# Splitting one kv product of a fused attention and MLP kernel by pair member, with casts and norms spread anew

## The chip, the cores and the metric

The kernel runs on one core of one Trainium2 chip. The metric is the device time of one execution in microseconds (us). Each kernel is run several times beside the kernel before on the same chip. Engines: PE is TensorE's matmul side and PEld its weight loads, ACT is ScalarE, DVE is VectorE, POOL is GpSimd, SP is the engine that issues the loads. Names in the profile lines: Eq and Ek are the exponentials of q and k, va is v after its cast, kvn is kv after its norm (the division by the sums), tp are the transposed queries and qT their copy, xT is the copy of x. A bank is one of PE's accumulator banks.

## The reference, cut to what matters

```python
def _attn_ref(q, k, v):                 # (8 batches, 8 heads, 576 rows, 64)
    q_s = softmax(q, axis=-1)           # per row
    k_s = softmax(k, axis=2)            # per column, over the 576 rows
    kv  = einsum('bhsd,bhse->bhde', k_s, v)
    return einsum('bhsd,bhde->bhse', q_s, kv)

def _moe_ref(x, w_in, w_out, beta):     # x: (4608, 512), w_in: 512 x 2048
    h = x @ w_in
    g = h * (1.0 / (1.0 + np.exp(-beta * h)))
    return g @ w_out
```

The softmax calls stand for the five lines each that the reference spells out. Inputs and output are float32.

## The kernel before

The kernel works through nine chunks of 512 rows. For each it forms kv of the heads, x (queries times kv), h (x times the first weight), tanh and g, and acc (g times the second weight). Batches 0 and 1 have a path of their own, since their data and both weights must first be loaded. Heads are handled in two halves `g`. Within a half, pair member `a` selects the PE row tile, and member `c` selects which 64 of 128 output rows are used.

The parts that the change and the argument touch:

```python
def ekv_mm(b, g, o0=0, c0=0, c1=VW - 2):        # VH = 66, VW = 132
    for t in range(KT9):                        # 9 row blocks
        for a in range(2):
            r = slice(a * KR, (a + 1) * KR)
            nc.tensor.matmul(ekv[b, 2 * g + a][:, o0 : o0 + c1 - c0],
                             Ek[b][r, t, g]..., ve(b)[r, t, g, c0:c1], ...)
def eks_mm(b, g):                               # the sums alone, two columns
    ekv_mm(b, g, VW, D, VH)
...
# the head: batch 0, second half of heads
ekv_open(0, 1, ("X1", "K"))
eks_mm(0, 1)
x_group(0, (0,), ["X0", "A0"])
ev_cast(0, 1, 0, nc.gpsimd)
ev_cast(0, 1, 1, nc.vector, 0, 5)
ev_cast(0, 1, 1, nc.gpsimd, 5, KT9)
ekv_rk(0, 1)
ekv_mm(0, 1)
x_out(0, 0, nc.scalar)
eq_out(0, 1, nc.vector)
...
ekv_norm(0, 1, nc.vector, nc.scalar)
x_out(0, 1, nc.vector)
for i in range(2):
    unit_mm(0, i, 0, 1)                         # two h matmuls as filler
x_group(0, (1,), ["X0", "H0"])
for i in range(2, 4):
    unit_mm(0, i, 0, 1)
...
def batch_1():                                  # the program order on ACT matters below
    b_mm(32)                                    # 32 of batch 0's 64 acc matmuls
    eq_exp(1, 0); eq_exp(1, 1)                  # exponentials of q
    eq_sum(1, 0); eq_div(1, 0, nc.vector)
    for c in range(2): ek_exp(1, 0, c)          # exponentials of k, first heads
    b_mm(20)                                    # emits output copies of tiles 0 and 1 on ACT
    eq_sum(1, 1)
    eq_t(1, 0, "X0", None)
    ...
    ev_cast(1, 0, 1, nc.scalar, 0, 4)
    eq_div(1, 1, nc.vector)
    for c in range(2): ek_exp(1, 1, c)          # exponentials of k, second heads
    b_mm(3)
    ekv_mm(1, 0)                                # the first kv product of batch 1
    b_mm(1)                                     # emits the output copy of tile 2 on ACT
    eq_t(1, 1, "H2", None)
    ekv_rk(1, 0, D)
    ekv_norm(1, 0, nc.vector, nc.scalar)
    eq_out(1, 0, nc.vector)                     # copy of qT
    ...
    b_mm(4)
    x_group(1, (0,), ["X0", "H0"])
    ekv_mm(1, 1)                                # the second kv product of batch 1
```

The softmax here doesn't subtract the row's maximum and nothing guards it: scores larger than these inputs give would overflow.

## Time and profile before

| | kernel before |
|---|---|
| median of the first three runs | 283.3 us (283.15 to 283.39) |
| span of the profiled run | 281.6 us |
| PE, ACT, DVE, POOL busy | 97%, 60%, 56%, 25% |
| DMA, mean over the span | 184 GB/s; 374 to 407 in the slices from 7 to 42 us |
| largest PE gap after the head | 0.32 us, ahead of batch 1's first kv product |

PE is busy throughout, so there is little to gain except in the first 16 us (the head, up to the dense stream of h) and where batch 1 joins. The lines that show this stand in the prediction.

### The profile page before, as it was taken

The page shows a single profiled execution, that of the slowest core. Times are in us where ns is not written, and L with a number is a line of the kernel's source. Part 1 is how long each engine was busy: PE and PEld are TensorE (multiplying, and loading weights), DVE is VectorE, ACT ScalarE, POOL GpSimd, SP SyncE. Part 2 cuts the span into 40 slices and gives each one's busy share as a digit, 9 for nine tenths or more (in the row PEclk, how much of TensorE's full clock was granted, in tenths as well). Part 3 has the DMA queues.
Part 4 walks back from the last instruction along what each step waited for, and adds up shares of the span by engine and source line. Part 5 has one row for each costly group of instructions (what it writes and reads, how often), then busy time and mean ns, then how long its engine had stood idle before and what let it go on. Part 6 is the DMA issues. An engine that isn't in the chain of part 4 may idle for free.

```text
span 281.6 us, 4611 instructions
## 1 busy us (share of the span) xinstructions
PE 273.1 (97%) x1664; PEld 136.1 (48%) x1692; DVE 156.8 (56%) x283; ACT 167.6 (60%) x279; POOL 70.3 (25%) x120
## 2 busy tenths in 40 slices
PE   7899999999999999999999999999999999999995
PEld 3555444545444445444544444444444444444444
DVE  2967369977865475549564766466453334444401
ACT  4757368867965587557855785478454544444411
POOL 3368721540721063104510361027000000000000
PEclk9999999999999999999999999999999999999999
DMA  7999999889699908991699069905100201031112
GB/s 233 374 391 407 389 384 358 303 161 359 158 217 350 199 37 182 331 240 52 154 331 279 26 135 300 284 29 120 70 37 2 76 37 40 0 76 37 40 75 75
DMA packets 51559, 51.69 MB, mean 184 GB/s; under 512 B 21068, under 2 KB 41932, under 8 KB 51536
## 3 DMA queue, kind: packets, MB, share of 16 engines
q1 hardware_dynamic: 51360, 51.33, 61.4%
q8 instruction: 13, 0.21, 0.3%
q14 instruction: 10, 0.08, 0.1%
q10 hardware_dynamic: 144, 0.07, 0.1%
q0 software_dynamic: 32, 0.01, 0.0%
HBM read 38.28 MB, written 9.44 MB: 169 GB/s over the span
## 4 chain that ended last, share of the span: by engine, by line
PE 83%; DMA 13%; ACT 1%; issue 1%; SPq 1%; ACTq 0%
PE acc L511 40%; PE h L459 39%; DMA k<-in_k_dram 7%; DMA wo<-in_moe_w_out_dram 4%; DMA wi<-in_moe_w_in_dram 2%; PE kv L386 2%; PE x L410 2%; PE kv L258 0%; ACT Ek L230 0%; SPq L105 0%; ACT o L540 0%; SPq L117 0%; PE xt L424 0%; PE tp L217 0%; ACT va L152 0%
## 5 line engine op out<-in xcount | busy, mean ns | idle before, releaser
L473 DVE SCALAR_TENSOR_TENSOR g<-th,h 128x512 bf16<-128x512 bf16 x144 | 97.3, 685 | 97.2 <-ACT th L471 97.0
L471 ACT ACTIVATE th<-h,beta_h 128x512 bf16<-128x512 f32 x144 | 97.1, 689 | 84.6 <-PE h L459 81.6
L511 PE MATMUL acc<-w_out_b,g 128*128 128x512 bf16 (+2 forms) x590 | 142.8, 368 | 1.7 <-issue 1.1
L459 PE MATMUL h<-xT,w_in_b 128*128 128x512 bf16 x503 | 127.4, 379 | 0.7 <-DVE xT L166 0.3
L459 PEld LDWEIGHTS <-w_in_b 128*128 128x128 bf16 x576 | 64.9, 113 | 61.1 <-issue 0.5
L511 PEld LDWEIGHTS <-g 128*128 128x128 bf16 x608 | 56.9, 98 | 63.9 <-issue 2.5
L317 POOL TENSOR_TENSOR Eq<-Eq,qz 128x512 bf16<-128x512 bf16 x24 | 25.1, 1048 | 84.4 <-issue 41.0
L540 ACT ACTIVATE o<-acc 128x512 f32<-128x512 f32 x34 | 20.0, 591 | 8.9 <-PE acc L511 7.4
L161 POOL TENSOR_SCALAR_AFFINE_SELECT va<-v 128x256 bf16<-128x256 f32 (+3 forms) x55 | 21.4, 424 | 14.1 <-DMA v<-in_v_dram 13.9
L357 ACT ACTIVATE Ek<-k 128x640 bf16<-128x640 f32 x24 | 17.6, 735 | 0.0
L459 PE MATMUL h<-xTt,w_in_b 128*128 128x512 bf16 x63 | 16.4, 379 | 0.1
L315 DVE TENSOR_REDUCE qz<-Eq 128x8 f32<-128x512 bf16 x24 | 16.2, 675 | 0.0
L307 ACT ACTIVATE Eq<-q 128x512 bf16<-128x512 f32 x24 | 14.6, 622 | 0.0
L166 DVE CAST xT<-x 128x512 bf16<-128x512 f32 x16 | 10.9, 684 | 0.1
L201 DVE TENSOR_REDUCE qz<-Eq 128x16 f32<-128x1024 bf16 x4 | 4.9, 1216 | 10.6 <-ACT Eq L194 10.6
L152 ACT CAST xT<-x 128x512 bf16<-128x512 f32 x16 | 9.3, 579 | 1.9 <-PE x L410 1.8
L161 POOL TENSOR_SCALAR_AFFINE_SELECT w_in_b<-wi 128x512 bf16<-128x512 f32 x16 | 9.5, 612 | 3.1 <-DMA wi<-in_moe_w_in_dram 2.9
L584 PE MATMUL warm<-zf 128*128 128x512 f32 (+1 forms) x14 | 8.3, 719 | 1.5 <-DVE zf L551 1.5
L194 ACT ACTIVATE Eq<-q 128x1024 bf16<-128x1024 f32 x4 | 4.2, 1056 | 9.3 <-DMA q<-in_q_dram 9.3
L343 POOL TENSOR_TENSOR Et<-Et,zt 128x512 bf16<-128x512 bf16 x4 | 4.2, 1041 | 21.0 <-DVE zt L342 15.6
L161 POOL TENSOR_SCALAR_AFFINE_SELECT w_out_b<-wo 128x1024 bf16<-128x1024 f32 x8 | 8.3, 1039 | 1.8 <-DMA wo<-in_moe_w_out_dram 1.7
L230 ACT ACTIVATE Ek<-k 128x576 bf16<-128x576 f32 x8 | 5.0, 675 | 2.0 <-DMA k<-in_k_dram 2.0
(52 smaller groups left out, 79.8 us busy)
## 6 DMA issues: line engine op xcount, KB each, us to landing
q<-in_q_dram SPq DMA_DIRECT2D x16, 512.0 KB, 6.3
out_dram<-o SPq DMA_DIRECT2D x31, 256.0 KB, 3.1
k<-in_k_dram SPq DMA_DIRECT2D x24, 320.0 KB, 7.3
v<-in_v_dram SPq DMA_DIRECT2D x24, 320.0 KB, 7.5
wo<-in_moe_w_out_dram SPq DMA_DIRECT2D x8, 512.0 KB, 10.7
wi<-in_moe_w_in_dram SPq DMA_DIRECT2D x6, 512.0 KB, 8.8
k<-in_k_dram SPq DMA_DIRECT2D x4, 576.0 KB, 9.0
v<-in_v_dram SPq DMA_DIRECT2D x6, 288.0 KB, 8.7
```

What stands on the lines that cost most here:

```text
L152: nc.scalar.copy(dst, src)
L161: nc.gpsimd.affine_select(out=dst, in_=src, pattern=[[0, n]], base=0, channel_multiplier=0, compare_op=ALU.is_equal, fill=fill0,)
L166: eng.tensor_copy(dst, src)
L307: nc.scalar.activation(by_pair(Eq[b], m).rearrange("p t h d -> p h t d"), ld["q", b, hf][:, a : a + 2, :].rearrange("p h (t d) -> p h t d" ...
L315: nc.vector.tensor_reduce(z, e, axis=AX.X, op=ALU.add)
L317: nc.gpsimd.tensor_tensor(e, e, z.unsqueeze(3).to_broadcast((P, NT, 2, D)), ALU.mult)
L357: nc.scalar.activation(Ek[b][:, :, h0:h1, :].rearrange("p t h d -> p h t d"), ld["k", b, hf][:, a : a + h1 - h0, :].rearrange("p h (t d) - ...
L459: nc.tensor.matmul(hs[n, i][:], w_in_b[:, kt, blk * CH + r : (blk + 1) * CH : 4], rhs_a(n, kt), start=(kt == 0), stop=(kt == KT - 1),)
L471: nc.scalar.activation(th[:], h[:], ACTF.Tanh, scale=beta_h[:, i // 4, i % 4 : i % 4 + 1])
L473: nc.vector.scalar_tensor_tensor(out=g[:], in0=th[:], scalar=1.0, in1=h[:], op0=ALU.add, op1=ALU.mult)
L511: nc.tensor.matmul(acc[n, st][:, c0:c1], gs[n, j][:, min(st, 3) * P : (min(st, 3) + 1) * P], w_out_b[:, j, c0:c1], start=(j == 0), stop=(j ...
L540: nc.scalar.activation(o[:], acc[n, st][:], ACTF.Copy, scale=0.5)
```

## The change

The intent is to let the head's second half of heads start sooner. The old kernel makes the sums with 18 two-column products, waits until both halves of v are cast, and runs one product of 130 columns. The new one runs a product of 65 columns (64 and the sums) behind each half of v, and each has banks of its own, so that one half is normalized while the other runs. One part of v's cast moves from DVE to ACT, the copy of qT moves ahead of DVE's reciprocals, the second half's norms both go to DVE, one x copy changes from DVE to ACT, the two filler h matmuls move behind the second x product, and the banks of the h tiles rotate in another order. Elsewhere, in batch 1 too, only the call is written anew and the product gets one column more (131 for 130).

```diff
-    def ekv_mm(b, g, o0=0, c0=0, c1=VW - 2):
+    def ekv_mm(b, g, names, cs=(0, 1)):
+        ps = [bank(n, [P, 2, VH], F32, ...) for a, n in enumerate(names)]
...
-    ekv_open(0, 1, ("X1", "K"))
-    eks_mm(0, 1)
+    ev_cast(0, 1, 0, nc.gpsimd)
+    eq_out(0, 1, nc.vector)
+    ekv_mm(0, 1, ("X1", "K"), (0,))
     x_group(0, (0,), ["X0", "A0"])
-    ev_cast(0, 1, 0, nc.gpsimd)
-    ev_cast(0, 1, 1, nc.vector, 0, 5)
-    ev_cast(0, 1, 1, nc.gpsimd, 5, KT9)
+    ev_cast(0, 1, 1, nc.scalar, 0, 4)
+    ev_cast(0, 1, 1, nc.gpsimd, 4, KT9)
     ekv_rk(0, 1)
-    ekv_mm(0, 1)
+    ekv_norm(0, 1, (nc.vector, nc.scalar), (0,))
+    ekv_mm(0, 1, ("A1", "H2"), (1,))
     x_out(0, 0, nc.scalar)
-    eq_out(0, 1, nc.vector)
...
-    ekv_norm(0, 1, nc.vector, nc.scalar)
-    x_out(0, 1, nc.vector)
-    for i in range(2):
-        unit_mm(0, i, 0, 1)
+    ekv_norm(0, 1, (nc.vector, nc.vector), (1,))
+    x_out(0, 1, nc.scalar)
     x_group(0, (1,), ["X0", "H0"])
-    for i in range(2, 4):
+    for i in range(4):
         unit_mm(0, i, 0, 1)
...
-            return ("H1", "H2", "A1", "A0", "K", "X1", "X0", "H0")[i % 8] if i < 12 else (
+            return ("H1", "X1", "K", "A1", "H2", "A0", "X0", "H0")[i % 8] if i < 12 else (
```

## The prediction

> **What bounds the kernel now.** I read the busy table first, then the chain that ended last, then the order of events around the two places where TensorE (PE) has gaps: the head of batch 0 and the start of batch 1. PE is busy 97% of a span of 281.6 us, so time can only come out of PE's few gaps or out of work taken off PE.
>
> ```profile
> PE 273.1 (97%) x1664; PEld 136.1 (48%) x1692; DVE 156.8 (56%) x283; ACT 167.6 (60%) x279; POOL 70.3 (25%) x120
> PE 83%; DMA 13%; ACT 1%; issue 1%; SPq 1%; ACTq 0%
> ```
>
> The second line is the chain by engine: 83% PE, but 13% DMA, about 37 us, and the chain in order of time says where that DMA part lies. Columns are start, length, what.
>
> ```profile
> 2.91 8.33 DMA k<-in_k_dram
> ...
> 11.26 6.88 DMA wi<-in_moe_w_in_dram
> ...
> 18.19 10.29 DMA wo<-in_moe_w_out_dram
> 28.49 10.89 DMA k<-in_k_dram
> 39.38 0.02 issue
> 39.41 1.26 ACT Ek L230 x2
> 40.66 0.97 ACT o L540 x2
> 41.63 0.30 ACT va L152
> 41.94 0.05 issue
> 41.98 0.68 PE kv L258 x18
> ```
>
> The reader is to see that from 2.9 to 39.4 us no engine is on the chain: it is one load after another, up to k of batch 1. From that landing the chain runs through ScalarE (two exponentials, two output copies, a cast of v) into PE's kv product of batch 1 at 41.98 us; from there on it is PE to the end. The stretch table says whether the loads could have been sooner (columns: stretch, length, busy time and count for each engine, clock, DMA share, GB/s):
>
> ```profile
> 6.00:12.00 6.00, 5.59 (x46) 2.95 (x45) 5.85 (x10) 4.58 (x7) 0.67 (x1) 1.00 1.03 379
> 12.00:18.00 6.00, 5.04 (x61) 2.80 (x60) 3.77 (x11) 2.81 (x7) 4.68 (x8) 1.00 1.04 383
> 18.00:24.00 6.00, 6.00 (x29) 3.16 (x28) 4.75 (x9) 4.84 (x8) 4.26 (x9) 1.00 1.04 392
> 24.00:30.00 6.00, 5.95 (x29) 3.08 (x28) 4.35 (x8) 4.50 (x8) 5.00 (x7) 1.00 1.03 410
> 30.00:36.00 6.00, 6.00 (x30) 2.72 (x28) 1.12 (x2) 0.34 (x1) 4.96 (x5) 1.00 1.05 380
> ```
>
> The DMA share is full in each, and the bytes agree: up to k of batch 1 the kernel loads, by the sizes in the table of DMA issues, 4 x 512 KB of q, 3 x 576 KB of k, 576 + 2 x 288 KB of v, and 4096 KB of each weight: 13,120 KB, 13.4 MB. From 2.9 to 39.4 us that is 368 GB/s. This landing is pinned by bandwidth, not by anything the head computes. PE's own record at that point:
>
> ```profile
> 38.73 1.67 PE L511 MATMUL acc<-w_out_b,g 128*128 128x512 bf16 x7
> 40.41 0.61 PE L217 MATMUL tp<-ident,Eq 128*128 128x128 bf16 x8
> 40.85 0.81 PE L511 MATMUL acc<-w_out_b,g 128*128 128x512 bf16 x3
> 41.98 0.68 PE L258 MATMUL kv<-va,Ek 64*128 64x130 bf16 x18 [0.32 <-ACT va L152]
> ```
>
> PE arrives 0.32 us before its operand. So PE already has slack against the loads here: work before 40 us that gets shorter only lengthens this gap, and work that gets longer is free up to about 0.3 us.
>
> **What the Trainium skill says.** (1) "DMA: Bandwidth & Descriptors", Specifications: a fabric ceiling of 435 GB/s and a vendor derate of 368 GB/s. The trace agrees with a ceiling in that region: 379 to 410 GB/s with the engines always busy. (2) The same page, Anatomy of one DMA: the DMA engines don't wait on semaphores; the issuing sequencer does. The trace agrees: SyncE waits on buffers and landings while the share stays full, so a buffer freed some tenths sooner or later does not show. (3) "ScalarE: Activation LUTs", What ACT_TABLE_LOAD costs: 186 ns + 0.833 ns an element for a copy. For 256 elements 399 ns; the trace has 405 for this very shape. (4) "PSUM — Partial Sum Buffer", PSUM bank collisions: two engines may not be on one bank and quadrant at once, which is why the two halves of kv get banks of their own; no collision is in the trace.
>
> **The change part by part.** Only batch 0's second half of heads and the bank order of its h tiles change; batch 1 is only respelled (its product is one column wider, 131 for 130: 36 matmuls, 18 in a row at some 20 to 38 ns each; under 0.02 us). The head before, to be compared:
>
> ```profile
> 13.09 0.36 PE L258 MATMUL kv<-va,Ek 64*128 64x2 bf16 x17 [0.34 <-ACT kvn L281]
> 13.38 0.41 PE L410 MATMUL x<-qT,kvn 64*64 64x512 bf16 x4
> 13.72 0.71 PE L258 MATMUL kv<-va,Ek 64*128 64x130 bf16 x18
> 14.47 0.59 PE L459 MATMUL h<-xT,w_in_b 128*128 128x512 bf16 x2
> 14.99 0.57 PE L410 MATMUL x<-qT,kvn 64*64 64x512 bf16 x4
> 15.82 0.41 PE L459 MATMUL h<-xT,w_in_b 128*128 128x512 bf16 x1 [0.26 <-DVE xT L166]
> ```
>
> Removed: the pass of 18 two-column matmuls that only made the sums (0.29 us to the next start at 13.38), and the full 130-column pass (0.6 us where nothing holds it: 41.98 to 42.60 in batch 1). Added: two passes of 18 x 65 columns, estimated between those two, 0.33 us each. PE work: 0.89 against 0.66, so 0.2 us less.
>
> The order in time, worked out with the durations of before. Half 0 needs banks X1 and K, and K is freed by ScalarE's last norm of batch 0's first heads, as before: 13.09. It also needs GpSimd's cast of v (start 12.05, 0.67 long: 12.72) and is in time. So it runs 13.09 to 13.42, then the first x product, to 13.76. ScalarE's new cast (256 elements, 0.40) runs 13.04 to 13.45 and GpSimd's 320 elements to some 13.2, so half 1 starts at 13.76 and its last result is there by about 14.2. Meanwhile VectorE copies qT at 12.66 to 13.33 (before: 13.63 to 14.30, between the reciprocals and the norms), has its reciprocals at 13.58 to 13.80 and its norm of half 0 by 14.1; ScalarE has its one by 14.15 and the first x copy (0.585) by 14.7. Half 1's two norms are both VectorE's, 0.60 for two: 14.25 to 14.85. The second x product thus starts at about 14.8 instead of 14.99, and h follows 0.42 later (46.65 to 47.07 is the same step in batch 1): 15.25.
>
> But two h matmuls that ran at 14.47, as filler, now come after. From 15.25 PE has 64 h matmuls at 0.216 us, 13.8 us, and ends h at 29.05. Before, acc starts at 29.02. The earlier x product (0.2 us) and the wait for VectorE's copy (0.26 us, gone since bank A0 is no longer needed by the fourth h tile) pay for the filler moved behind (2 x 0.216 = 0.43). **Sum for the head: 0.0 us, give or take 0.3.** Then 52 acc matmuls lead to the transposes at 40.4, and the gap of 0.32 us before 41.98 takes up the rest: ScalarE's start there is k's landing at 39.4, and neither output copy ahead of the cast is late (both accumulations end by about 39.7). **Sum for the whole: 0.0 us.**
>
> The rotation of the h banks: tiles 4 to 7 now sit in H2, A0, X0, H0, all read out by 16 us and used from 18.7; tile 15's bank H2 is that of tile 4 instead of tile 9. The first accumulators X1 and K, taken from 29 us on, were last tiles 9 and 10 instead of 5 and 4; their g's run from 25.19, four in 2.48 us, so are done by 27.7. No new wait.
>
> **The rivals.** First: *the shorter head comes through.* If the gap in batch 1 were set by something that moves with PE, a gain of some 0.2 to 0.5 us would reach the end: 282.8 to 283.1. For it speaks only that the x product and its wait do get shorter; against it the chain above, where PE is not on the path before 41.98. Second: *the head gets longer.* If the 65-column passes cost nearly what the 130-column pass does (0.6 each, so +0.54), if ScalarE's cast waits for v or the two norms one after the other on VectorE are later than I have them, h ends 0.5 us later; less the gap of 0.32, the end is 0.2 later: 283.5. Third: *a bank freed late* stalls the h or acc stream for up to a tile's readout, about 1.4 us (0.69 for tanh, 0.68 for g): of which 0.3 is absorbed, so up to 284.4; the times above leave over 1 us to each, so I hold it for unlikely. Fourth: *the loads move.* A weight buffer freed later by a cast (v's second unit at 13.45 instead of 13.23) could delay an issue, but the share is full for ten microseconds at a time and each load takes 7 to 11 us from issue to landing, so it is hidden.
>
> **Range and chances.** The middle is the time before, 283.3. The three runs before lie between 283.15 and 283.39; with 0.2 us for another chip session and the first two rivals at about 0.3 to each side, the range is 282.8 to 283.8. Two per cent is 5.7 us: more than all PE gaps of the head together, and more than any stall that I can construct without a deadlock; so 98% within 2%, 1% on either side.
>
> **What would show each step.** Right: k of batch 1 lands at 39.4 as before; PE's kv of batch 1 starts at 42.0, behind ScalarE's cast of v, with a gap of between 0 and 0.6 us before it; acc starts at 29.0 within 0.3; the second x product starts at about 14.8; the copy of qT stands before the reciprocals; two passes of 65 columns follow at about 0.33 us. The prediction is wrong if kv of batch 1 starts 0.3 us or more off 42.0, if k lands elsewhere, or if new waits on g, th or norms turn up between 16 and 40 us.

## The result, and the profile after

The changed kernel took 283.36 us in the median of four runs (283.16 to 283.81), the kernel before 283.23 (283.15 to 283.39). The ratio is 1.0006, 95% interval 0.9989 to 1.0024. Ratios are the mean time of one kernel's fast runs over that of the other's of the same rounds, so they are not quite the ratio of the medians quoted. The times are the same, as predicted.

The run that was profiled is the slowest of the four (283.81 us, span 282.1). Its busy table and its chain by engine, from the page of the changed kernel:

```profile
PE 273.7 (97%) x1664; PEld 136.2 (48%) x1692; DVE 155.5 (55%) x282; ACT 168.1 (60%) x280; POOL 70.5 (25%) x120
PE 83%; DMA 13%; ACT 1%; issue 1%; SPq 1%; ACTq 0%
```

One DVE instruction fewer and one ACT instruction more: a cast of v and an x copy went to ACT, and a norm went to DVE. The chain in order of time, changed kernel (start, length, what):

```profile
28.99 10.90 DMA k<-in_k_dram
...
39.91 1.26 ACT Ek L230 x2
41.17 0.97 ACT o L538 x2
42.13 0.30 ACT va L152
...
42.49 0.69 PE kv L259 x18
```

It is the same chain as before, 0.5 us later: k of batch 1 lands 0.5 us later, and everything behind it moves by 0.5 us, as does the span (281.6 to 282.1). The head on PE, changed kernel (start, length, engine, line, operation, in brackets the wait before it):

```profile
12.39 0.75 PE L259 MATMUL kv<-va,Ek 64*128 64x65 bf16 x18
13.08 0.41 PE L408 MATMUL x<-qT,kvn 64*64 64x512 bf16 x4
13.42 0.45 PE L259 MATMUL kv<-va,Ek 64*128 64x65 bf16 x18
14.27 0.58 PE L408 MATMUL x<-qT,kvn 64*64 64x512 bf16 x4 [0.41 <-ACT xT L152]
15.03 1.24 PE L457 MATMUL h<-xT,w_in_b 128*128 128x512 bf16 x5 [0.17 <-issue]
```

The two passes of 65 columns are there, and the second x product starts at 14.27 instead of 14.99. Of its four matmuls only the first runs then: the weight loads of the other three wait for DVE's norms.

```profile
14.45 0.11 PEld L408 LDWEIGHTS <-kvn 64*64 64x64 bf16 x3 [0.55 <-DVE kvn L281]
```

The stream of h, 64 matmuls long, starts at 15.03. It did not end sooner for it: in this run PE then met weights that were not yet cast (PE again, later in time):

```profile
20.39 0.41 PE L457 MATMUL h<-xT,w_in_b 128*128 128x512 bf16 x1 [0.23 <-POOL w_in_b L161]
20.95 8.61 PE L457 MATMUL h<-xT,w_in_b 128*128 128x512 bf16 x38 [0.16 <-POOL w_in_b L161]
```

That cast waited for its load: it started at 19.72, in the kernel before at 18.19. So acc started at 29.39, in the kernel before at 29.02.

Two things are open after this one pair of profiles: whether the 0.5 us in the loads goes with the change, and whether the head got shorter at all.

### The profile page after: what moved, and what is told of

Same layout as the page of the kernel before. It is cut to its first block, busy times and chain, and to the rows that moved or that the text cites. A ratio compares the mean times of both kernels' runs of the same rounds, so it can differ in the third digit from the quotient of the medians.

```text
span 282.1 us, 4611 instructions
## 1 busy us (share of the span) xinstructions
PE 273.7 (97%) x1664; PEld 136.2 (48%) x1692; DVE 155.5 (55%) x282; ACT 168.1 (60%) x280; POOL 70.5 (25%) x120
## 4 chain that ended last, share of the span: by engine, by line
PE 83%; DMA 13%; ACT 1%; issue 1%; SPq 1%; ACTq 0%
PE acc L509 40%; PE h L457 39%; DMA k<-in_k_dram 7%; DMA wo<-in_moe_w_out_dram 3%; DMA wi<-in_moe_w_in_dram 3%; PE kv L384 2%; PE x L408 2%; PE kv L259 0%; ACT Ek L230 0%; SPq L105 0%; ACT o L538 0%; SPq L117 0%; PE xt L422 0%; PE tp L217 0%; ACT va L152 0%
## 5 line engine op out<-in xcount | busy, mean ns | idle before, releaser
L166 DVE CAST xT<-x 128x512 bf16<-128x512 f32 x15 | 10.3, 685 | 0.6 <-PE x L408 0.5
L582 PE MATMUL warm<-zf 128*128 128x512 f32 (+1 forms) x14 | 9.0, 778 | 1.5 <-DVE zf L549 1.5
L408 PE MATMUL x<-qT,kvn 64*64 64x512 bf16 x64 | 6.0, 391 | 0.4 <-ACT xT L152 0.4
## 6 DMA issues: line engine op xcount, KB each, us to landing
wo<-in_moe_w_out_dram SPq DMA_DIRECT2D x8, 512.0 KB, 10.4
```

The lines of the kernel that those rows point to most:

```text
L166: eng.tensor_copy(dst, src)
L408: nc.tensor.matmul(xps[b, 2 * g + c][o, :], kvn[b][r, j, :], qT[b][r, g, a] if b < EARLY else qT[b][r, :, j, :], start=True, stop=True,)
```

## The experiments

Two groups of numbers recur. "acc starts" is the start of batch 0's first acc matmul, the end of PE's h stream. "The second kv product" is batch 1's `ekv_mm(1, 1)`, after which PE runs without a gap that matters.

### The changed kernel again: do the loads come later with it?

No edit.

> The changed kernel once more, untouched. Its first profile had every load from the fourth weight unit on land 0.5 us later than in the kernel before (k of batch 1 at 39.88 against 39.38), and its span was 0.5 us longer. Theory A (the end is set by the landing of batch 1's loads; the head's work is hidden by them): the ratio is 1.000 within 0.001, and in the new profile the span differs from 282.1 by just as much as k's landing differs from 39.88; kv of batch 1 starts 2.6 us after that landing. Rival B (the change itself makes the loads later, by some buffer that comes free later): k lands at 39.9 again and the kernel is slower by 0.3 to 0.5 us in the mean of five.

Measured: 283.35 us median (283.02 to 283.68, 5 runs), kernel before 283.17 (9 runs), ratio 0.9998 (0.9980 to 1.0016). In this profile k's exponentials started at 39.14, earlier even than in the kernel before (39.41). Rival B falls: the lateness belongs to the run and not to the change.

One part of theory A's expectation failed, though. The first kv product started at 41.91, which is 2.77 us after k's exponentials and not 2.6, and there was no gap on PE before it, because acc had started late (29.50). And the span was 281.3, shorter by 0.8 us than in the first profile, where k's landing accounts for 0.77. So PE was late at the first kv product and it cost nothing. Something later must still have been waited for.

### One load left out, in both kernels: does the head show when the loads are out of the way?

```diff
     for blk in range(1, 4):
         load_w_in(blk, 0, 2)
-        load_w_in(blk, 2, 4)
+        if blk == 1:
+            ld["wi", 1, 2] = (ld["wi", 1, 0][0], 4)   # the first half's tile again
+        else:
+            load_w_in(blk, 2, 4)
```

The results are wrong (relative error 0.52).

> The kernel before, with one 512 KB load left out (the second half of the second block of the first weight; its cast reads the first half's tile again, so the result is wrong on purpose). Every later load has 1.35 us less ahead of it. Theory A: k of batch 1 lands at about 38.0, the gap of 0.32 us before kv of batch 1 closes, kv starts at about 41.65 and the time falls by 0.3 us (282.9 to 283.1), not by 1.35, because PE arrives at 41.65 at the earliest. Rival (the loads do not matter at all): kv of batch 1 stays at 42.0 and the time at 283.3.

> The changed kernel with the same load left out (wrong on purpose). Theory A with a head that is really shorter on PE: without the loads in the way the head's gain comes through; h ends at about 28.85, kv of batch 1 starts at about 41.45, and the time is 0.2 us (0.1 to 0.4) under that of the kernel before with the same load left out, 0.4 to 0.7 under 283.3. Rival C (the head did not get shorter on PE, my sum of 0.0): both kernels with the load left out take the same time within 0.1 us.

Measured: 282.59 us (282.55 to 282.67, ratio 0.9972) for the kernel before, and 282.10 us (282.00 to 282.57, ratio 0.9959) for the changed one. Both got faster, so the loads do matter; the kernel before by 0.6 us in the medians and 0.8 by the ratio (interval 0.3 to 1.3), which is more than the first gate's 0.3. In its profile k landed at 38.86 and not at 38.0 as expected, and the second kv product came 0.53 us sooner (44.54 against 45.07). The 0.5 us between them is in the direction that I expected, but not for the reason: acc started at 28.98 and 28.94, so the heads are equal, as rival C has it, though the equal times that rival C forecast did not come. What differed is the landing. k's exponentials started at 38.88 and at 38.05.

In the changed kernel with one load less PE waits for nothing at this point. PE, start and length, that kernel:

```profile
43.64 0.41 PE L408 MATMUL x<-qT,kvn 64*64 64x512 bf16 x4
44.02 0.69 PE L259 MATMUL kv<-va,Ek 64*128 64x131 bf16 x18
```

and the changed kernel with all loads:

```profile
44.91 0.73 PE L408 MATMUL x<-qT,kvn 64*64 64x512 bf16 x4
45.57 0.69 PE L259 MATMUL kv<-va,Ek 64*128 64x131 bf16 x18
```

The x product is 0.41 us long in the first and 0.73 in the second: 0.32 us of waiting are hidden inside a group of four matmuls that the chain of waits counted as PE's work. Here is the later gate. ACT's stream in the kernel before shows what is waited for:

```profile
42.42 1.26 ACT L230 ACTIVATE Ek<-k 128x576 bf16<-128x576 f32 x2 [0.49 <-DMA k<-in_k_dram]
43.58 0.58 ACT L540 ACTIVATE o<-acc 128x512 f32<-128x512 f32 x1
44.06 0.61 ACT L281 ACTIVATE kvn<-kv,rks 64x64 bf16<-64x64 f32 x2
```

PE's weight loads for the x product, kernel before, name what ended each wait:

```profile
44.41 0.10 PEld L410 LDWEIGHTS <-kvn 64*64 64x64 bf16 x1 [0.43 <-DVE qT L166]
44.73 0.11 PEld L410 LDWEIGHTS <-kvn 64*64 64x64 bf16 x3 [0.21 <-ACT kvn L281]
```

The two norms of the first heads stand in program order behind the exponentials of the second heads, which wait for k's second load, and behind an output copy. The x product needs the norms.

To see whether the 0.5 us between the pair goes with the kernel, the pair was run again on another chip:

> The kernel before with one load left out, a second time (wrong on purpose). The first time it ended 0.5 us after the changed kernel with the same load left out, and the profiles put that down to the landing of q and k of batch 1 (k at 38.86 against 38.03), not to PE (acc started at 28.98 and 28.94). If that landing is a matter of the session, the pair is now within 0.2 us of each other or the other way round; if it goes with the kernel, k lands 0.8 us later here than in the changed kernel again, and the time is 0.5 us longer again. In either case the span is 236.4 to 236.5 us after the start of batch 1's second kv product.

> The changed kernel with one load left out, a second time, beside the one before. PE alone allows the second kv product of batch 1 at about 44.0, so 282.1 us is the floor; with loads as late as in the other kernel the first time it takes 282.6.

Measured: 282.23 us (281.95 to 282.76, ratio 0.9958) for the kernel before, 282.31 us (282.12 to 282.67, ratio 0.9960) for the changed one. They are the same. So the 0.5 us does not go with the kernel. The first pair had been measured in one session on one chip, side by side, so the session alone does not explain it either; what set the two landings there stays open.

### More PE work in the head

The changed kernel with two warm-up products more, and the kernel before with one:

```diff
+    dummy(2, CH)
     ekv_mm(0, 1, ("A1", "H2"), (1,))
```

```diff
+    dummy(1, CH)
     ekv_mm(0, 1)
     x_out(0, 0, nc.scalar)
```

> The changed kernel with two of the warm-up products more (about 1.9 us of PE work, four records of some 0.5 us) ahead of the second half's kv product in the head. Theory A: the first 0.4 to 0.8 us are taken up by the gaps behind (0.33 before kv of batch 1, 0.1 before the transposes, up to 0.4 at the weight casts), so the time rises by 1.1 to 1.5 us, and the gap before kv of batch 1 is gone. Rival D (PE is the path from the head on): plus 1.9 us.

> The kernel before with one warm-up product more (0.96 us of PE, two records) ahead of the second half's kv product in the head. Six profiles so far have the span at 236.4 to 236.5 us after the start of batch 1's second kv product, and that product, where PE is not late, 2.67 us after k's second half of batch 1 starts its exponential. Theory A2 (two gates: k's first half before the first kv product, k's second half, through ScalarE's exponentials, an output copy and two norms, before the x product and the second kv product; the second gate is the later one by about 0.4 us): PE's true slack in the kernel before is about 0.74 us (0.32 at the first gate and some 0.42 more at the second), so the time rises by 0.2 us (0 to 0.4). Theory A as predicted (the first gate alone, slack 0.32): plus 0.64. Rival D (PE is the path): plus 0.96.

Measured for the two: 284.68 us (284.42 to 284.93), ratio 1.0045 (1.0028 to 1.0063), which is 1.3 us more than the changed kernel on that chip, for 1.91 us of added work. The second kv product went from 44.80 to 46.21. Some 0.6 us were absorbed, within what theory A had put (a rise of 1.1 to 1.5). This rules out rival D, but it does not tell one gate from several; and the two profiles differ in the form of the head (see the last section but one), so their difference is not the added work alone.

Measured for the one: 283.76 us (283.42 to 284.00), kernel before 283.30, ratio 1.0010 (0.9996 to 1.0023). In its profile acc started at 30.03, 1.01 us later than in the profile before, and the second kv product still stood 2.66 us behind k's second exponentials, as far as without the added work, to 0.01 us. In this profiled execution PE's delay was absorbed whole. The 0.39 us by which that product came later (45.46 against 45.07) is k's landing in that run (exponentials at 42.80 against 42.42). The mean of the six runs rose by about 0.3 us, as theory A2 of the expectation (two gates) has it, and allows anything from 0 to 0.65. It excludes rival D (0.96) and, by a hair only, does not exclude the 0.64 of the single gate; the profile does.

### Taking the gate away, with right results

First the output copy of tile 2 is emitted behind the norms and the cast:

```diff
-            if j == NJ - 1 and (n, st) != (0, 3):
+            if j == NJ - 1 and (n, st) not in ((0, 2), (0, 3)):
                 store(n, st)
...
         ev_cast(1, 1, 1, nc.scalar, 3, 6)
+        store(0, 2)
```

> The changed kernel with one output copy of batch 0 (tile 2, 0.58 us on ScalarE) emitted after the two norms of batch 1's first heads and the cast of v, instead of before them. It changes nothing in the head and nothing in the loads. Theory A2: the norms come 0.5 us sooner, the x product then waits only for VectorE's copy of qT, the second kv product starts 0.3 us sooner and the time falls by 0.3 us (0.2 to 0.45) below the changed kernel, in the range of 282.9 to 283.1 where that is at 283.3. Theory A as predicted (the first gate alone sets the end): no change, within 0.1.

Then in addition ACT's cast of v goes ahead of the other two output copies, in the changed kernel and in the kernel before:

```diff
+        ev_cast(1, 0, 1, nc.scalar, 0, 4)
         b_mm(20)
         eq_sum(1, 1)
         eq_t(1, 0, "X0", None)
...
-        ev_cast(1, 0, 1, nc.scalar, 0, 4)
```

> As the one before, and ScalarE's cast of v of batch 1 is moved ahead of the two output copies as well, so that the first kv product does not wait for them (about 0.5 to 0.6 us sooner at the first gate). Theory A2: little more than the deferred copy alone gives, within 0.15 us of it, since the second gate and VectorE's chain from q (division, norms, copy of qT) stay where they are. Theory A as predicted (the first gate sets the end): the time falls by 0.3 us beyond that of the deferred copy alone.

> The same two moves on the kernel before. If the head is the same length on PE in both kernels (acc started at 28.98 and 28.94 us in the two profiles with a load left out) or is hidden anyway, this takes the same time as the changed kernel with the two moves, within 0.15 us. If the head is really shorter by 0.2 us or more and now comes through, this one is slower by that.

Measured, six runs each: the deferred copy 283.14 us (282.83 to 284.03, ratio 0.9997, 0.9980 to 1.0014); both moves on the changed kernel 283.07 us (283.03 to 283.24, ratio 0.9988, 0.9976 to 1.0001); both moves on the kernel before 282.90 us (282.80 to 284.06, ratio 0.9993, 0.9974 to 1.0011). By the times alone the first is inconclusive, and the fall of 0.3 us below the changed kernel that was expected of it is not shown by them. By the means the second lies 0.24 us below the first (283.10 against 283.34), more than the 0.15 that theory A2 allowed; by the medians it is 0.07, and two of the first one's six runs stand at 283.9 and 284.0, so this too is open by the times. ACT in the profile of the deferred copy shows the norms directly behind the exponentials:

```profile
43.30 1.26 ACT L230 ACTIVATE Ek<-k 128x576 bf16<-128x576 f32 x2 [0.49 <-DMA k<-in_k_dram]
44.47 0.61 ACT L279 ACTIVATE kvn<-kv,rks 64x64 bf16<-64x64 f32 x2
```

The second kv product followed k's second exponentials by 2.39 us (45.69 less 43.30) instead of 2.65. That is the 0.26 us that was to be had; k landed 0.9 us later in that run than in the profile of the kernel before and hid it. The third run shows what is waited for next. PE's weight loads for the x product, kernel before with both moves; now all four wait for the copy of qT and none for ACT's norms:

```profile
44.24 0.11 PEld L410 LDWEIGHTS <-kvn 64*64 64x64 bf16 x4 [0.42 <-DVE qT L166]
```

DVE's chain from q (sum, reciprocal and product of the first heads, the same of the second, then norm and copy of qT) starts with q's landing, and it is the next gate. Old and new head take the same time here too: means of 283.15 and 283.10.

Both moves on the changed kernel were run once more, on a third chip:

> The changed kernel with the two moves on ScalarE in batch 1, a second time, to see whether it is faster than the kernel before at all. By the profiles the second kv product now waits for q's landing (8.39 us after q's exponential starts, in three profiles) instead of k's (8.67 after it in the kernel before): 0.28 us less, so a ratio of 0.9990, with landings that differ by some 0.5 us from run to run around it.

Measured: 283.03 us (282.86 to 283.61), kernel before 283.45, ratio 0.9988 (0.9970 to 1.0005). Twice the same ratio. Weighting the two by their intervals gives 0.9988, with a half-width of about 0.0010, so it is likely faster than the kernel before, by 0.3 us. Each interval alone touches 1.

### All thirteen profiles in one sum

Three delays, one constant each, fit every profile. PE alone: the second kv product starts 15.08 us after acc starts, taken from the four profiles in which nothing else is late. q: 8.39 us after q's first exponential starts, from the four without the k gate. k: 2.65 us after k's second exponentials start, while the output copy stands before the norms. The latest of the three should be the start measured, and the span should be that plus a constant. (The first gate, which the prediction named, is k's first load: exponentials plus 2.57 to the first kv product, plus 2.67 to the second. For the kernel before that gives 39.41 + 5.24 = 44.65; it is the latest in none of the profiles.)

| profile | PE: acc + 15.08 | q + 8.39 | k + 2.65 | measured | span less measured |
|---|---|---|---|---|---|
| before | 29.02: 44.10 | 36.40: 44.79 | 42.42: **45.07** | 45.07 | 236.5 |
| changed | 29.39: 44.47 | 36.90: 45.29 | 42.92: **45.57** | 45.57 | 236.5 |
| changed, again | 29.50: 44.58 | 36.14: 44.53 | 42.15: **44.80** | 44.80 | 236.5 |
| before, a load less | 28.98: 44.06 | 35.86: 44.25 | 41.89: **44.54** | 44.54 | 236.4 |
| changed, a load less | 28.94: **44.02** | 35.04: 43.43 | 41.05: 43.70 | 44.02 | 236.4 |
| before, a load less, again | 29.45: **44.53** | 35.03: 43.42 | 41.03: 43.68 | 44.53 | 236.4 |
| changed, a load less, again | 29.03: **44.11** | 35.27: 43.66 | 41.26: 43.91 | 44.12 | 236.4 |
| changed, two products more | 31.12: **46.20** | 36.37: 44.76 | 42.47: 45.12 | 46.21 | 236.5 |
| before, one product more | 30.03: 45.11 | 36.87: 45.26 | 42.80: **45.45** | 45.46 | 236.5 |
| changed, copy deferred | 29.78: 44.86 | 37.30: **45.69** | gate removed | 45.69 | 236.5 |
| changed, both moves | 29.52: 44.60 | 36.45: **44.84** | gate removed | 44.84 | 236.5 |
| before, both moves | 28.91: 43.99 | 36.24: **44.63** | gate removed | 44.63 | 236.5 |
| changed, both moves, again | 29.45: 44.53 | 36.42: **44.81** | gate removed | 44.81 | 236.5 |

No row is off by more than 0.01 us. The three constants were taken from these same profiles, each from those in which its gate comes last, so the close fit is in part built in. What is not built in is that one constant serves four or five profiles each, that the other gates come out earlier in every row, and that the span follows the product by 236.4 to 236.5 us whichever gate was last. In the kernel before PE's own path ends 0.97 us before it is needed, and in the changed one 1.10 us. This slack is not a property of the kernel: in the second profile of the changed kernel, with a late head and an early k, it is 0.22 us.

## Why the prediction was right

**The time and the main reason.** The end is set by loads that run at full rate, and the head's work ends before it matters. The table shows it, and taking one load out shows it by intervention: PE's path is the latest in three of the four profiles with a load less, and otherwise only where two products were added to it. k's exponentials started at 38.30 in the mean of those four profiles and at 39.54 in the mean of the nine with all loads; the 1.25 us between them is close to the 1.35 that the missing load was put at. The rates of 379 to 410 GB/s that the prediction shows lie above the 368 that it quotes as a derate, so that figure is no ceiling here.

**What was luck.** That the median came within 0.1 us of the forecast is partly luck: single runs of the kernel before went from 282.98 to 284.63 in the later sessions, and the profiled run of the changed kernel (283.81) lies just outside the range that was stated. That the two kernels take the same time is not luck.

**The sum of 0.0 us for the head** held. Among profiles without an added product or a wait for weights within the h stream, acc starts at 28.91 to 29.02 with the old head and at 28.94 and 29.03 with the new one. Where the head is in its late form (next section but one), it starts at 29.45 with the old head and at 29.45 to 29.52 with the new one (the deferred copy's 29.78 again has waits for weight casts in it). The second x product does start sooner, and the h stream does start sooner than its 62 remaining matmuls did, but the two filler matmuls come back behind it, as the prediction worked out.

**The steps in the head.** The copy of qT stands before the reciprocals, and the passes of 65 columns take 0.36 and 0.37 us from start to next start (read from the starts of the weight loads: 12.72, where a wait within the pass ends, to 13.08, and 13.42 to 13.79) against an estimate of 0.33. The second x product was put at 14.8 and h at 15.25; measured were 14.27 and 15.03 in the first profile, where the whole head ran some 0.35 us earlier, and 14.61 and 15.34 in the run with a load less. What it waited for was in part as I had it: its first matmul waited for ACT's copy of the first x tile, which held the bank, and the other three, to 14.45, for DVE's norms (the same in both profiles). No new wait came from the rotation of the h banks.

**What was mis-sized.** The prediction took the gap of 0.32 us ahead of the first kv product for PE's whole slack, and said that from there on it is PE to the end. That step failed. A second and a third gate follow within 3.1 us, the slack in that profile is 0.97 us, and the gap that is seen is only the first part of it. The rest stood as longer durations of merged PE groups (x product 0.72 instead of 0.41) and was counted as PE's in the chain. The error did no harm since the added slack only made the head matter less, but the prediction's second rival ("less the gap of 0.32, the end is 0.2 later") would have been sized wrong, and the profile with one more product shows it: 1.01 us of delay, absorbed whole.

**What the prediction would have called wrong.** It named a first kv product 0.3 us or more off 42.0, k landing elsewhere, and new waits on g, th or norms as signs of an error. The first two showed in the first profile (42.49 and 39.88); the new waits there (0.23 and 0.16 us) were for weight casts, which it had not named. They were not the change's doing: the landing moved back in the next profile. The marks were set tighter than the kernel repeats itself.

## What to carry to other kernels

When the chain of waits has a stretch of back-to-back loads at full rate, compute the rate from bytes and landing times first; work ahead of the landing that such loads pin can be rearranged and the time will not move, as long as the work stays within its slack (here 0.2 to 1.1 us in the profiles of the two kernels as they are). Count the slack to the last gate and not to the first gap that is seen: look at every load that lands near the join, at the program order of each engine behind it, and compare the durations of merged groups with those of the same group elsewhere, because waits hide inside them. Where gates lie 0.3 us apart, as here, removing one can gain only the distance to the next.

## What the runs showed of the hardware that was not expected

The head has two forms, in both kernels, 0.5 us apart. It depends on whether POOL's first cast of v or DVE's second product of the exponentials of q starts first. POOL and DVE in the kernel before, on time:

```profile
9.77 0.67 POOL L161 TENSOR_SCALAR_AFFINE_SELECT va<-v 128x576 bf16<-128x576 f32 x1 [6.27 <-DMA v<-in_v_dram]
9.92 1.59 DVE L205 TENSOR_TENSOR Eq<-Eq,qz 128x1024 bf16<-128x1024 bf16 x1
```

and in the second run of the changed kernel with both moves, late:

```profile
10.14 1.52 POOL L161 TENSOR_SCALAR_AFFINE_SELECT va<-v 128x576 bf16<-128x576 f32 x1 [6.64 <-DMA v<-in_v_dram]
9.90 1.22 DVE L205 TENSOR_TENSOR Eq<-Eq,qz 128x1024 bf16<-128x1024 bf16 x1
```

DVE's product starts at 9.88 to 10.01 in all thirteen profiles; POOL's cast starts when v lands, at 9.42 to 10.27, so v's landing decides. Whichever starts second is stretched: DVE from 1.22 to 1.59 us, or POOL from 0.67 to 1.52. (In the first profile of the changed kernel v landed so early, at 9.42, that the two overlap by only 0.13 us, and the product keeps its 1.22.) In the five late profiles the cast ends 0.52 to 0.54 us after DVE's product, in the eight others the product ends 1.07 to 1.09 after the cast. The Trainium skill says this in "SBUF — State Buffer", section "SBUF: two separate sides": a DVE operation with two SBUF inputs and a GpSimd operation that reads SBUF exclude each other, and the first to start holds the ports for the whole instruction. The traces agree, and PE's kv product waits for that cast: it started at 11.7 to 11.8 in the five late profiles against 10.4 to 11.0 in the eight others. The prediction had overlooked the 1.59. Four of the eight profiles of the changed kernel and its variants are late and one of the five of the kernel before; that is too few to say that they differ, and the order is settled before any instruction that the change moved. No experiment reordered the two; with all loads present the 0.5 us would have been hidden, by the sum above.

The same loads do not land at the same time from run to run. Among the nine profiles with all loads, k's first exponentials started at 39.14 to 40.29 us. Yet the bytes moved from 6 to 39.4 us agree between the first profiles of the two kernels within 0.1%, by the stretch table. Which transfer finishes when is what varies. Why it does stays open.

## What the Trainium skill lacked or had wrong

- "DMA: Bandwidth & Descriptors": no section says how far the landing of one transfer can move while the total rate stays the same. Here it was 1.15 us (39.14 to 40.29, by the exponentials that wait for it) for a load of 576 KB; the DMA share from 6 to 39.4 us is full (1.04) in all nine profiles. This is more than the effect under study.
- "Perfetto Trace Analysis" and the other pages do not deal with views that merge a run of matmuls into one row, as the view used here does. In such a row waits lie inside the duration: the same four x matmuls read 0.41 us in one profile and 0.73 in another with no idle time named in PE's row; only the rows of the weight loads carry the waits. This belongs to the view and not to the chip.
- "TensorE: Matmul & The Clock Gate", section "Wait — 56ns, not 53.3ns?", gives about 25 ns as the least time from start to start of small matmuls. Here 17 products of two columns, each with its own weights and alternating between two row tiles, took 0.29 us from the first start to the next group's (13.09 to 13.38, 17 ns each), and 18 of 65 columns 0.37 us (21 ns each). The sentence does not except row tiles that alternate. The same page does treat tiles that overlap, under "Part 3: Packing small matmuls — row/col tiling", but gives no spacing for a stream that alternates between two tiles with new weights each time.
